# Two attentions on one core: the first group's Q and K, in halves by turns

## The chip, the cores and the metric

The kernel runs on one core of a Trainium2 chip. The metric is the device time in microseconds of one execution, as the median of several runs. Durations and waits come from one further execution, taken with the hardware profiler.

## The reference, cut to what matters

Two independent attention layers, A and B, each on 2048 tokens of 1024 features with 32 heads of 32, all in fp32. Both compute `qkv = x @ wqkv`, attention per head, and `o @ wo`; the outputs are put side by side.

```
B: scores = (q @ k.T) * Dh**-0.5 ; key in the last 256 tokens, else -1e9 ; softmax ; @ v ; @ wo
A: W, dil = 8, 2 ; idx = pos[:, None] - arange(W) * dil      # 8 keys, two tokens apart
   logits = einsum("bhsd,bhswd->bhsw", q, kg) * Dh**-0.5 ; masked ; softmax ; @ vg ; @ wo
```

In layer A a token only looks at tokens an even distance away, so the even and the odd tokens are two separate sequences of 1024, each with a window of 8 neighbours.

## The kernel before, in words

**Units and groups.** The work is cut into eight units of 512 tokens, `u` = 0 to 7. Units 0 to 3 are layer B (`DU` = 4, "dense"), units 4 to 7 are layer A. In each unit the 32 heads form eight groups of four, `s` = 0 to 7. A group's Q has 128 columns, and so has its K.

**Matmuls.** Every fp32 factor is split into a high and a low half (type fp32r): a cast gives the high half (L276 on ACT or L279 on DVE) and a subtraction on DVE the low one (L282). Each product then takes three matmuls (`TERMS`: high x high, high x low, low x high). Q or K of one group is a sum over eight blocks `k` of 128 features (`NK` = 8), so 24 matmuls of 512 columns into one PSUM bank. `qk_items` (L568) makes 16 items of three matmuls for a group, eight of Q and then eight of K; the last item of each evacuates its bank (L583 `evac_window` in layer A: L586 for Q, L591 for K). V is made by `v_items` (L728) in parts; the last part of a unit (two groups of heads) has 16 items on two banks, and its last two items copy these out to `vbuf` through `copy_out` (L718; L720 on ACT or L723 on DVE, whichever the planner holds to be sooner). In layer A, `window` (L1176) makes the scores of a group (128 small matmuls), the softmax on DVE and ACT (the band), eight copies of the turned band into `wide` (L1263, L1266) and the values block, whose result ACT copies at L1336.

**Banks and buffers.** Q, K, V and output products share a ring of three PSUM banks, tag `g` (`Ring`, L534; `psg` has 7 - `NS` = 3 buffers). A new product takes the next bank in turn, and its first matmul waits until the former content is evacuated. Weights lie in `wpool` (three buffers), x in `xpool` (nine tiles, each a high and a low half of one `k` block; a unit uses eight, two for each of four loads), raw loads in `raws` (three buffers).

**What sets the order.** One Python loop (at the end of the function) writes one program for all engines. It holds four lists: `gemm` (all items of Q, K, V and the output products, in a fixed order), scores, values and small auxiliary items. A `Clock` keeps planned times of every engine; at each step the loop takes the item whose planned start is earliest, a list of scores or values ahead of `gemm` when equal, and emits its instructions. What an item sets off on ACT, DVE, POOL and SP is emitted at that point or at a planned later time (`defer`). So the order on each engine follows from planned times, and on the chip each engine runs its program in that order, waiting on semaphores. Scores of the next group are released `P_LATE` = 1.5 us (planned) after the last copy of the band of the group before.

**Loads.** `Stream` (L177) holds one list of loads (`items`) in order of use. POOL issues each load into a raw buffer as soon as one is free (L221); `split_to` (L225) emits the cast and subtraction into the final tile. At the start of units 5 and 6 the list has: Q's weights of group 0, x quarters 0 and 1, K's weights of group 0, x quarters 2 and 3 (each quarter holds two of the eight `k` blocks). `x_items` (L1165) splits the four quarters; these four items are spliced among the 16 items of the last V part of the unit before, ahead of its items 1, 5, 9 and 13 (counted from 0), since they take over that unit's x tiles as V leaves them. In `run` of `qk_items` (L683) the items of K with `k` = 2 and `k` = 5 ask for the weights that come next.

The lines that a sentence can't say, from the loop that fills `gemm`:

```
            elif V_SLOTS.get(NG - 1) == p[2] and 0 < p[1] < U - 1:
                m = 2 * VPARTS[p[2]][1]
                for g, x in reversed(list(enumerate(x_items(p[1] + 1)))):
                    new[m * g + XAT:m * g + XAT] = x
```

Of the kernel before, what the change touches and what calls it, by code (L numbers as in the profile page):

```python
# [16 lines left out]
NK = 8  # L17
# [274 lines left out]
def kernel(ctx, tc, xs, wqk, wv, wo, outs, units):  # L292
# [3 lines left out]
    U = len(units)  # L296
    DU = sum(u[2] for u in units)
# [867 lines left out]
    def x_items(u):  # L1165
        xt[u], xready[u] = [], []

        def run(g):
            a, b = st.get(where["x", u, g])
            xt[u] += a  # L1170
            xready[u] += b

        return [[(lambda: 0.0, lambda g=g: run(g), 0.0, lambda: None)] for g in range(4)]
# [376 lines left out]
    def fill(at, n):  # L1550

        def run():
            mm(ps, idle[:, :P], idle, start=True, stop=True)

        def after(last):
            if last:
                rs.give(bank, ck.now + ck.SEM)

        return [(lambda: 0.0, run, CG, lambda i=i: after(at == FILL[-1][0] and i == n - 1)) for i in range(n)]
# [10 lines left out]
    for p in plan:  # L1570
        if not marks and p[1:] == (DU, 2) and p[0] == "qk":
            marks.append(len(gemm))
        if len(marks) == 1 and p[0] == "p":
            marks.append(len(gemm))
        if p[0] == "qk":
            new = qk_items(p[1], p[2])
            if p == ("qk", 0, 0):
                q, k, x = new[:NK], new[NK:], x_items(0)
                f = dict(FILL)
                new = x[0] + sum([q[i:i + 1] + fill(i + 1, f.get(i + 1, 0)) for i in range(4)], [])  # L1580
                for i in (1, 2, 3):
                    new[new.index(q[2 * i]) if i < 2 else len(new):0] = x[i]
                    if i == 1:
                        new += k[:4]
                    else:
                        new += q[2 * i:2 * i + 2] + k[2 * i:2 * i + 2]
            if p[1:] == (0, NG - 1):
                x1 = x1 or x_items(1)
                for g in range(3, FIRST_X - 1, -1):
                    new[NK + 2 * g - 2:NK + 2 * g - 2] = x1[g]  # L1590
            gemm += new
        elif p[0] == "v":
            new = v_items(p[1], p[2])
            if p[1:] == (0, 2) and FIRST_X:
                x1 = x_items(1)
                for g in range(FIRST_X - 1, -1, -1):
                    new[X1_AT[g]:X1_AT[g]] = x1[g]
# [4 lines that stand above are left out]
            gemm += new  # L1602
        elif p[0] == "o":
            gemm += o_items(p[1], p[2])
        elif p[0] == "p":
            gemm += product(p[1], p[2])
        elif p[0] == "vp":
            new = value_product(p[2])
            if VP_AT.get((p[1], NG - 1)) == p[2:] and p[1] + 1 < U:
                for g, x in reversed(list(enumerate(x_items(p[1] + 1)))):  # L1610
                    new[4 * g + XAT:4 * g + XAT] = x
            gemm += new
# [87 lines left out]
```

## Time and profile before

| | |
|---|---|
| median of 3 runs | 1789.3 us (1788.56 to 1789.42) |
| profiled execution, its own time | 1788.09 us |
| its span, first to last instruction | 1786.4 us |
| granted TensorE clock, mean | 1.000 |
| HBM read and written | 201.33 MB and 53.48 MB |
| bytes moved by DMA | 324.57 MB, mean 182 GB/s |

The profile page gives shares of the span for each engine: PE (matmuls), PEld (weight loads, which overlap them), DVE, ACT and POOL. Matmuls are pipelined and their ends are modelled, so two successive matmuls of 512 columns show a length of about 393 ns each but start closer together than that. A timeline row is: start in us from the start of the span, length in us, engine, source line, operation, output<-inputs by the program's names with sizes, count, and in brackets the idle time just before with what ended it. All matmuls have one line (L324, a helper), so they are told apart by names: `g<-x,w` of 512 columns are Q or K, `g<-w,x` are V (256 columns in the last part of a unit, 512 in the wide part), `s<-pbuf` the scores and `o<-wide,vbuf` the values of layer A. The stretches of this study are the starts of units 5 and 6, near 1144 and 1321 us of the span.

### The profile page before, as it was taken

Reading aid. Unit: us, or ns where it says so; the run is one execution under the profiler, and the core shown is the slowest. Engines: PE = TensorE matmul, PEld = TensorE weight load, DVE = VectorE, ACT = ScalarE, POOL = GpSimd, SP = SyncE. Lnnn points to the kernel's source line nnn. Section 1 sums busy time; section 2 is a strip of 40 time slices with the busy share of each in tenths; the row PEclk is TensorE's granted clock in tenths of the full one; section 3 lists DMA queues with packets and bytes.
Section 4 is the critical chain, followed back from the end, with each engine's and each line's share of the span. In section 5 each row is a group of like instructions: output and inputs, shape, how many; then the busy total and the mean of one; then the engine's idle time right before and its main releaser. Section 6 shows DMA issues by size and latency. Waiting matters only on the chain.

```text
span 1786.4 us, 38443 instructions
## 1 busy us (share of the span) xinstructions
PE 1768.4 (99%) x14496; PEld 1440.2 (81%) x14496; DVE 1295.5 (73%) x2881; ACT 936.9 (52%) x2332; POOL 412.8 (23%) x962
## 2 busy tenths in 40 slices
PE   9999999999999999999999999999999999999999
PEld 7787778888777888778788788878888887877887
DVE  6777876768867769867669546566577868767866
ACT  5565566555656565655654524444354546455442
POOL 3322324222333233242323410110011101001210
PEclk9999999999999999999999999999999999999999
DMA  8354664645645556555556255656576758948984
GB/s 256 106 151 136 187 167 137 163 135 152 186 142 154 154 127 173 150 148 156 133 142 186 72 181 180 210 193 209 175 219 197 233 169 290 303 151 271 310 319 144
DMA packets 154793, 324.57 MB, mean 182 GB/s; under 512 B 18032, under 2 KB 58992, under 8 KB 154608
## 3 DMA queue, kind: packets, MB, share of 16 engines
q0 software_dynamic: 45792, 166.74, 30.3%
q1 hardware_dynamic: 98736, 137.02, 26.9%
q10 hardware_dynamic: 10080, 18.35, 2.8%
q8 instruction: 115, 1.88, 0.4%
q14 instruction: 70, 0.57, 0.1%
HBM read 201.33 MB, written 53.48 MB: 143 GB/s over the span
## 4 chain that ended last, share of the span: by engine, by line
PE 92%; DVE 2%; DMA 2%; ACT 2%; issue 1%; SPq 0%; ACTq 0%; DVEq 0%; POOLq 0%
PE g L324 72%; PE s L324 13%; PE o L324 7%; DMA raw<-xs 1%; DVE w L282 1%; ACT s L1403 0%; DMA raw<-sd 0%; DMA pbuf<-nat 0%; DMA raw<-wqk 0%; DVE x L282 0%; ACT w L276 0%; DMA raw<-sx 0%; DMA qst<-nat 0%; ACT wide L1263 0%; ACT x L276 0%
## 5 line engine op out<-in xcount | busy, mean ns | idle before, releaser
L324 PE MATMUL g<-x,w 128*128 128x512 f32 x3552 | 875.8, 393 | 2.9 <-ACT x L276 1.0
L324 PEld LDWEIGHTS g<-x,w 128*128 128x128 f32 x3552 | 655.9, 188 | 131.7 <-issue 6.6
L282 DVE TENSOR_TENSOR w<-raw,w 128x512 fp32r<-128x512 f32 x510 | 334.3, 697 | 53.5 <-ACT w L276 47.2
L1398 DVE CUSTOM_DVE_ANT_0 s<-s,mask_d 128x384 f32<-128x384 f32 (+2 forms) x512 | 261.8, 554 | 98.4 <-PE s L324 98.1
L1403 ACT ACTIVATE s<-s,nm 128x384 f32<-128x384 f32 (+2 forms) x512 | 274.3, 537 | 109.9 <-DVE nm L1398 103.3
L324 PE MATMUL g<-w,x 128*128 128x256 f32 (+1 forms) x1728 | 306.9, 327 | 0.9 <-DVE w L282 0.7
L1462 POOL TENSOR_SCALAR_AFFINE_SELECT pbuf<-pbuf 128x128 f32<-128x128 f32 (+1 forms) x605 | 220.1, 392 | 315.7 <-ACT pbuf L1483 313.6
L324 PEld LDWEIGHTS g<-w,x 128*128 128x128 f32 x1728 | 255.3, 190 | 26.3 <-DVE w L282 2.2
L324 PE MATMUL g<-r,w 128*128 128x512 f32 x960 | 238.4, 393 | 0.5 <-DVE r L1362 0.5
L1483 ACT ACTIVATE pbuf<-s 128x384 f32<-128x384 f32 (+2 forms) x480 | 203.4, 504 | 65.3 <-PE s L324 63.5
L324 PEld LDWEIGHTS g<-r,w 128*128 128x128 f32 x960 | 177.2, 188 | 36.0 <-DVE r L1362 1.1
L221 POOL DMA_DIRECT2D raw<-wqk x126 | 68.4, 543 | 388.9 <-DVE w L282 265.2
L324 PEld LDWEIGHTS s<-qst,kst 128*128 128x128 f32 x704 | 113.5, 188 | 42.2 <-ACT s L1403 16.9
L324 PE MATMUL s<-kst,qst 96*128 96x384 f32 (+2 forms) x512 | 142.2, 342 | 0.9 <-ACT s L1403 0.7
L324 PE MATMUL s<-qst,kst 128*128 128x256 f32 (+2 forms) x704 | 137.0, 301 | 4.0 <-ACT s L1403 3.2
L279 DVE CAST w<-raw 128x1024 fp32r<-128x1024 f32 x176 | 121.3, 689 | 8.8 <-PE g L324 7.9
L324 PEld LDWEIGHTS s<-kst,qst 96*128 96x128 f32 x512 | 93.6, 189 | 26.2 <-issue 4.5
L276 ACT CAST w<-raw 128x1024 fp32r<-128x1024 f32 (+1 forms) x80 | 82.4, 1037 | 51.7 <-PE g L324 16.0
L1403 ACT ACTIVATION_READ_ACCUMULATOR s<-s,nm 128x1 f32 x512 | 105.3, 206 | 0.0
L1263 ACT COPY wide<-band 32x512 f32<-32x512 f32 x128 | 79.0, 617 | 30.3 <-DVE band L1254 28.8
L324 PE MATMUL o<-pbuf,vbuf 128*32 128x384 f32 (+2 forms) x1408 | 91.1, 388 | 0.0
L625 ACT ACTIVATE nat<-g 128x512 fp32r<-128x512 f32 x64 | 38.3, 598 | 97.7 <-PE g L324 87.1
(90 smaller groups left out, 1426.6 us busy)
## 6 DMA issues: line engine op xcount, KB each, us to landing
raw<-wqk POOLq DMA_DIRECT2D x126, 512.0 KB, 4.6
raw<-wv POOLq DMA_DIRECT2D x60, 512.0 KB, 4.8
qst<-nat SPq DMA_DIRECT2D x96, 256.0 KB, 4.2
kst<-nat SPq DMA_DIRECT2D x96, 256.0 KB, 5.5
raw<-wo POOLq DMA_DIRECT2D x44, 512.0 KB, 4.4
raw<-xs POOLq DMA_DIRECT2D x28, 512.0 KB, 4.5
kst<-halo SPq DMA_DIRECT2D x72, 128.0 KB, 4.5
pbuf<-nat SPq DMA_DIRECT2D x128, 65.0 KB, 3.2
```

The source lines that it names most:

```text
L221: (self.nc.scalar if early else self.nc.gpsimd).dma_start(raw if len(ap.shape) == 2 else raw.rearrange("p (a b) -> p a b", a=2), ap)
L276: nc.scalar.copy(t[:, 0, :], raw)
L279: nc.vector.tensor_copy(t[:, 0, :], raw)
L282: nc.vector.tensor_tensor(t[:, 1, c:c + 512], raw[:, c:c + 512], t[:, 0, c:c + 512].bitcast(F32), op=ALU.subtract)
L324: nc.tensor.matmul(out, left, right, **k)
L625: nc.scalar.activation(hl[:, 0, :], ps, AF.Copy, scale=sc)
L1263: nc.scalar.copy(diag[r:r + 32, :, :, c:c + 32], turned[r:r + 32, :, :, 1, :])
L1398: nc.vector.tensor_tensor_reduce(ps[:, :n], ps[:, :n], mask[:, cut:full], scale=-1.0, scalar=BIG, op0=ALU.add, op1=ALU.min, accum_out=nm)
L1403: nc.scalar.activation(ps[:, :n], ps[:, :n], AF.Exp, bias=nm, scale=-1.0, accum_out=sm)
L1462: nc.gpsimd.affine_select(w, w, pattern=[[0, m], [step, n]], compare_op=ALU.is_ge, fill=0.0, base=base, channel_multiplier=chan)
L1483: nc.scalar.activation(w, ps[:, :pack * n].rearrange("p (j n) -> p j n", j=pack), AF.Exp)
```

## The change

For the first group of heads (`s` = 0) of units 5 and 6, the 16 items of Q and K are put in another order: Q's `k` = 0 to 3, K's `k` = 0 to 3, Q's `k` = 4 to 7, K's `k` = 4 to 7. Two accumulations are then open at a time, in two banks. The items themselves, the loads and their order, and the places where x is spliced are as before.

```
                         new += q[2 * i:2 * i + 2] + k[2 * i:2 * i + 2]
+            if DU < p[1] < U - 1 and p[2] == 0:
+                new = [new[c + i] for h in (0, NK // 2) for c in (0, NK) for i in range(h, h + NK // 2)]
             if p[1:] == (0, NG - 1):
```

## The prediction

> **What bounds the kernel now.** I read the page first: busy shares, granted clock, chain by engine.
>
> ```profile
> PE 1768.4 (99%) x14496; PEld 1440.2 (81%) x14496; DVE 1295.5 (73%) x2881; ACT 936.9 (52%) x2332; POOL 412.8 (23%) x962
> PEclk9999999999999999999999999999999999999999
> PE 92%; DVE 2%; DMA 2%; ACT 2%; issue 1%; SPq 0%; ACTq 0%; DVEq 0%; POOLq 0%
> ```
>
> TensorE is busy 99% of the span and makes 92% of the chain. The change removes no matmul, so all it can alter is waits of TensorE, and of those only the few where layer A's second and third unit (u = 5 and 6) begin. I looked for these places in the timeline of PE and then of PEld. A row is: start, length, instruction, count, and in brackets the idle time ahead of it with its releaser.
>
> PE at the start of unit 5, then of unit 6:
>
> ```profile
> 1132.23 11.68 PE L324 MATMUL g<-w,x 128*128 128x256 f32 x96
> 1143.75 4.27 PE L324 MATMUL g<-x,w 128*128 128x512 f32 x18
> 1148.97 0.50 PE L324 MATMUL g<-x,w 128*128 128x512 f32 x1 [0.95 <-ACT x L276]
> 1149.97 6.90 PE L324 MATMUL g<-x,w 128*128 128x512 f32 x29 [0.51 <-DVE x L282]
> 1156.71 0.84 PE L324 MATMUL g<-w,x 128*128 128x512 f32 x3
> 1157.49 1.32 PE L324 MATMUL s<-pbuf 32*32 32x40 f32 x128
> 1158.73 1.12 PE L324 MATMUL o<-wide,vbuf 128*32 128x136 f32 x32
> 1159.79 2.58 PE L324 MATMUL g<-w,x 128*128 128x512 f32 x10
> 1162.84 17.34 PE L324 MATMUL g<-w,x 128*128 128x512 f32 x74 [0.47 <-DVE w L282]
> ```
> ```profile
> 1321.09 11.07 PE L324 MATMUL g<-x,w 128*128 128x512 f32 x48
> 1331.99 1.52 PE L324 MATMUL g<-w,x 128*128 128x512 f32 x6
> ```
>
> The 96 matmuls of 256 columns are V's last part of unit 4. Behind them stand 18 + 1 + 29 = 48 of g<-x,w: 24 of Q, then 24 of K, three for each of eight k-blocks. Unit 6 runs its 48 without a break, in 1331.99 - 1321.09 = 10.90 us, 0.227 each. Unit 5 needs 1156.71 - 1143.75 = 12.96, so it loses 2.06 us. It stops after 18 matmuls, that is ahead of Q's k = 6, whose x is the last fetched quarter: first for the ACT half (L276), then for the DVE half (L282). **The stall that the change aims at exists, once: 2.06 us at unit 5 and none at unit 6.**
>
> Next, ACT in the same places, since all that feeds or frees the matmuls here passes it:
>
> ```profile
> 1143.29 1.05 ACT L276 CAST w<-raw 128x1024 fp32r<-128x1024 f32 x1 [0.17 <-DMA raw<-wqk]
> 1144.47 1.14 ACT L276 CAST x<-raw 128x512 fp32r<-128x512 f32 x2
> 1148.30 1.14 ACT L276 CAST x<-raw 128x512 fp32r<-128x512 f32 x2 [2.68 <-DMA raw<-xs]
> 1149.34 1.06 ACT L720 COPY vbuf<-g 128x512 f32<-128x512 f32 x2
> 1151.44 0.60 ACT L586 ACTIVATE nat<-g 128x512 f32<-128x512 f32 x1 [1.04 <-PE g L324]
> 1151.94 0.60 ACT L1263 COPY wide<-band 32x512 f32<-32x512 f32 x1
> ...
> 1156.91 0.59 ACT L591 COPY nat<-g 128x512 f32<-128x512 f32 x1 [1.25 <-PE g L324]
> ...
> 1159.92 0.59 ACT L1336 COPY r<-o 128x512 f32<-128x512 f32 x1 [2.21 <-PE o L324]
> 1160.41 2.94 ACT L276 CAST w<-raw 128x1024 fp32r<-128x1024 f32 x3
> ```
> ```profile
> 1322.98 1.14 ACT L276 CAST x<-raw 128x512 fp32r<-128x512 f32 x2 [2.57 <-DMA raw<-xs]
> 1324.02 1.06 ACT L720 COPY vbuf<-g 128x512 f32<-128x512 f32 x2
> ```
>
> V's last matmul ends at 1132.23 + 11.68 = 1143.91, yet V's two banks are copied out (L720) only from 1149.34. ACT is not busy meanwhile: it sits idle 2.68 us for the DMA of the last x quarter, because the last quarter's item of x_items(u + 1) is spliced ahead of V's item 13 (of 0 to 15), so these two casts stand ahead of the copies in ACT's program. Unit 6 shows the same: idle 2.57, casts at 1322.98, copies at 1324.02.
>
> **The change, part by part.** No instruction is added or removed; 32 items of three matmuls are reordered, as Q k 0-3, K k 0-3, Q k 4-7, K k 4-7.
>
> *Q's k 4-7 later by 12 matmuls.* At unit 5 Q's k = 6 would come after 30 matmuls, 1143.75 + 30 x 0.227 = 1150.56, behind the 1149.97 at which its x is complete. That stall goes: at most -2.06 us.
>
> *K's k 0 earlier, and with it K's bank.* Here a new wait comes up. The ring of g banks has three (7 - NS). V's two blocks hold two, Q takes the third, so K's first matmul needs V's first bank, which the first L720 frees. Before, K began after Q's 24 matmuls, behind that copy. Now it is due after 12.
> - Unit 5: due at 1143.75 + 12 x 0.227 = 1146.47. The copy starts at 1149.34 and lasts half of the pair's row and a little (0.59), to 1149.93; from the end of the cast (1148.30 + 0.62) to the matmul that waited for it (1148.97) are 0.05 us, so K starts at about 1149.97. That is a wait of 3.5 us, with the rest of Q and K queued behind it in PE's order. By chance it is the instant at which the old kernel went on; but there 29 matmuls were left and here 36. Net **7 x 0.227 = +1.59 us**.
> - Unit 6: due at 1321.09 + 12 x 0.227 = 1323.81. The copy ends at 1324.02 + 0.58 = 1324.60, K starts at 1324.65: **+0.83 us**, where nothing was lost before.
>
> The other end for both is that the copy does not hold K: -2.06 and 0. I take the held value, since copies and casts are emitted before any of the moved items, so ACT's order up to there can't change. K's weights are no obstacle: cast at 1143.29 to 1144.34, their DVE halves done by the row below at 1145.66, ahead of 1146.47.
>
> ```profile
> 1144.37 1.29 DVE L282 TENSOR_TENSOR w<-raw,w 128x512 fp32r<-128x512 f32 x2 [0.45 <-ACT w L276]
> ```
>
> *What stands behind unit 5's K.* In the old order three matmuls of the next V part precede the score block (1157.49); then come the values block, ACT's copy of its result (1159.92), three weight casts (1160.41) and DVE's halves, for which PE waits until 1162.84. The planner releases the scores 1.5 us after the eight band copies (L1263, L1266). Q's evacuation (L586), ahead of those copies so far, falls behind them as Q ends later, so the scores come due by up to one evacuation (0.6 us) sooner, while K ends later in the plan. I expect the block right behind K, one V item (three matmuls, 0.69 us) earlier. The wait at 1162.84 hangs on the values block, so it moves by 1.59 - 0.69 = +0.90 and what PE does in between is absorbed. Bounds for unit 5 are +0.90 and +1.59; I take **+0.90**.
>
> *Nothing from the rest.* The next weights are asked for at K's k = 2 and 5, earlier in PE's order; Q's weight buffer comes free 12 matmuls later in the order, near 1155.4, and its next user is cast at 1160.41, five microseconds of cover. Q's bank is wanted again only after K and another block. The x tiles are read until K's k = 7, as before. On POOL and SP no DMA moves except the rows of Q and K, which go out as much later as their evacuation; the score block that reads them is a group away. Without that cover the price would be the shift itself, 1.6 us.
>
> *The sum.* +0.90 + 0.83 = +1.73 us. The profiled execution took 1788.09 us (span 1786.4, and 1.7 around it), so 1789.8 by its own time; the median of the three runs is 1789.3, 1.2 above, and gives **1791.0 us**, +0.10%.
>
> **The rivals.**
>
> *K is not held.* The copies come ahead of the casts, or the bank is another. Then -2.06 at unit 5 and nothing at unit 6: 1787.2. For it: the ring is small and I count its turns by hand. Against it: the 2.68 us of idle ACT between V's end and L720. Chance 0.10.
>
> *The loss is absorbed further on.* Where the chain of waits does not run through PE, a late PE costs nothing.
>
> ```profile
> 1471.65 7.68 issue
> 1479.33 0.01 POOLq L221
> 1479.35 4.60 DMA raw<-sx
> ```
>
> If this stretch starts from something other than PE, the 1.73 us are swallowed: 1789.3. Against it: PE is 149.72 of 150 us busy from 1350 to 1500, so there is little to swallow them.
>
> ```profile
> 1350.00:1500.00 150.00, 149.72 (x2018) 121.21 (x2016) 117.71 (x218) 74.94 (x142) 17.89 (x33) 1.00 0.68 210
> 1600.00:1786.40 186.40, 181.03 (x1294) 147.62 (x1292) 135.93 (x223) 82.89 (x133) 31.65 (x55) 1.00 0.76 259
> ```
>
> Chance 0.10.
>
> *The clock drops in the new gap (the slower side).* The longest idle time of PE around these places is 0.95 us, and the clock column stands at 1.00 throughout; the new gap at unit 5 would be 3.5 us from due to start, 3.1 without the last matmul's own 0.4. If the granted clock halved behind it, each matmul would cost 0.227 more. Eight of them take the sum past 0.2% (1.73 + 8 x 0.227 = 3.55); twelve, K's first half, give +2.7: 1793.7. Nothing in the trace speaks for it, as no such gap is in it. Chance 0.08. The Trainium skill, "TensorE: Matmul & The Clock Gate", section "Why this matters for your kernels", asks for no idle gap over about 3 us between bursts, since one idle window sends the clock to half. By it the gap is just at the edge; its window (3.4 us, in Part 1) at half speed would cost some 1.7 us more, an estimate from that page. No run here shows it.
>
> *The order behind it shifts.* The planner writes one order for all engines, and a changed due time may put score blocks or casts elsewhere for the rest. The price is bounded by waits that hang on that order: PE idles 186.40 - 181.03 = 5.4 us after 1600. Half as much again: +2.7 on the forecast, 1793.7, chance 0.14, and more, not less, if it hits several places; all of it gone: 1785.6, chance 0.04; no net effect, 0.02.
>
> **How the numbers follow.** Forecast 0.52 (with unit 5 between +0.90 and +1.59: 1791.0 to 1791.7). A difference below 0.2%, 3.6 us, is about what a measurement of this kernel can't tell from none. Slower by more: clock 0.08 and order 0.14, together 0.22. Faster by more: order 0.04. The same: 0.52 + 0.10 + 0.10 + 0.02 = 0.74. The range 1787.0 to 1794.0 takes in the free bank, the absorbed loss and the plain prices of clock and order, and leaves out the faster order and the upper part of the slower two.
>
> **What would show it.** In the changed trace, at unit 5: 12 matmuls of g<-x,w, a wait of about 3.5 us released by ACT vbuf L720, then 36 in one piece; no wait on x L276. At unit 6: 12, a wait of some 0.8 us on the same, then 36. ACT: still idle for raw<-xs ahead of L720; L586 behind the band copies. The score block right behind K. The clock at 1.00. I am wrong if K's first matmul follows Q's twelfth without a wait, if L720 stands ahead of the last casts, or if PE's busy time in the stretches behind 1350 moves by more than unit 5 and 6 do.

## The result, and the profile after

| | before | after |
|---|---|---|
| median of 14 runs each | 1788.57 us (1786.98 to 1791.97) | 1793.39 us (1790.58 to 1795.88) |
| ratio, 95% interval | | 1.0026 (1.0019 to 1.0033) |
| profiled execution, own time | 1788.09 us | 1794.82 us |
| its span | 1786.4 us | 1793.1 us |

The change costs 4.65 us by the ratio (3.4 to 5.9; the two medians lie 4.82 apart). The forecast was 1791.0, +1.73 us: the right sign and inside the range, but the loss is 2.7 times as large, and past the 0.2% behind which "the same" ended.

The page of after: busy time by engine, and the group of Q's and K's matmuls (busy time and mean ns of one | idle time ahead of them and what ended most of it).

```profile
PE 1771.4 (99%) x14496; PEld 1441.4 (80%) x14496; DVE 1294.8 (72%) x2879; ACT 939.1 (52%) x2334; POOL 411.7 (23%) x962
L324 PE MATMUL g<-x,w 128*128 128x512 f32 x3552 | 878.3, 393 | 5.4 <-ACT vbuf L720 4.0
```

All matmuls are still there. Of the 5.4 us for which Q and K kept PE idle, 4.0 now end with V's copy at L720, the release that the prediction named. DVE has two instructions fewer than before and ACT two more (2881 and 2332 then), so some of the planner's choices changed too.

PE of after at the start of unit 5, then of unit 6:

```profile
1143.74 2.91 PE L324 MATMUL g<-x,w 128*128 128x512 f32 x12
1149.35 10.05 PE L324 MATMUL g<-x,w 128*128 128x512 f32 x36 [2.71 <-ACT vbuf L720]
1159.24 0.84 PE L324 MATMUL g<-w,x 128*128 128x512 f32 x3
1160.02 1.32 PE L324 MATMUL s<-pbuf 32*32 32x40 f32 x128
...
1323.58 2.91 PE L324 MATMUL g<-x,w 128*128 128x512 f32 x12
1327.78 8.48 PE L324 MATMUL g<-x,w 128*128 128x512 f32 x36 [1.30 <-ACT vbuf L720]
1336.10 2.20 PE L324 MATMUL g<-w,x 128*128 128x512 f32 x9
1338.23 1.32 PE L324 MATMUL s<-pbuf 32*32 32x40 f32 x128
```

ACT of after in the same places:

```profile
1147.68 1.14 ACT L276 CAST x<-raw 128x512 fp32r<-128x512 f32 x2 [2.35 <-DMA raw<-xs]
1148.72 1.06 ACT L720 COPY vbuf<-g 128x512 f32<-128x512 f32 x2
1156.72 0.60 ACT L586 ACTIVATE nat<-g 128x512 f32<-128x512 f32 x1 [1.57 <-PE g L324]
...
1326.11 1.14 ACT L276 CAST x<-raw 128x512 fp32r<-128x512 f32 x2 [3.16 <-DMA raw<-xs]
1327.15 1.06 ACT L720 COPY vbuf<-g 128x512 f32<-128x512 f32 x2
```

The picture is the forecast one: twelve matmuls, a wait for L720, which stands behind casts that wait for x, then 36 in one piece. At unit 5 the first copy ends near 1148.72 + 0.59 = 1149.31, and K starts at 1149.35.

Two things were not forecast as likely. First, the 36 matmuls of unit 5 last 1159.24 - 1149.35 = 9.89 us, not 36 x 0.227 = 8.17. The windows of after tell why (length, then busy us and instructions of PE, PEld, DVE, ACT, POOL, then the granted clock, the DMA share and GB/s):

```profile
1149.30:1151.00 1.70, 1.65 (x5) 1.36 (x6) 1.70 (x3) 1.26 (x3) 0.46 (x1) 0.72 0.97 380
1151.00:1152.00 1.00, 1.00 (x4) 0.73 (x3) 1.00 (x3) 0.85 (x2) 0.26 (x1) 0.50 1.01 359
1152.00:1153.00 1.00, 1.00 (x4) 0.81 (x3) 0.60 (x2) 0.96 (x4) 0.00 (x0) 0.50 1.03 167
1153.00:1154.00 1.00, 1.00 (x4) 0.82 (x4) 0.00 (x0) 0.98 (x3) 0.72 (x1) 0.77 0.91 373
1154.00:1156.00 2.00, 2.00 (x10) 1.65 (x9) 0.00 (x0) 1.13 (x3) 0.00 (x0) 1.00 0.71 163
```

The clock fell to half some 0.7 us behind the gap and stayed there for about 3.4 us (0.28 x 1.7 / 0.5 + 2 + 0.23 / 0.5), which costs half of that, 1.7.

Second, more was lost behind unit 6. All waits of PE between 1345 and 1530, first before, then after:

```profile
1497.50 1.12 PE L324 MATMUL o<-wide,vbuf 128*32 128x136 f32 x32 [0.28 <-ACT wide L1266]
1501.76 0.58 PE L324 MATMUL s<-pbuf 32*32 32x40 f32 x41 [0.66 <-issue]
1515.69 0.50 PE L324 MATMUL g<-w,x 128*128 128x512 f32 x1 [0.19 <-DVE w L279]
1516.42 0.73 PE L324 MATMUL g<-w,x 128*128 128x512 f32 x2 [0.22 <-DVE w L282]
```
```profile
1477.62 2.37 PE L324 MATMUL g<-x,w 128*128 128x512 f32 x9 [0.66 <-issue]
1502.86 1.12 PE L324 MATMUL o<-wide,vbuf 128*32 128x136 f32 x32 [0.76 <-ACT wide L1266]
1507.46 0.57 PE L324 MATMUL s<-pbuf 32*32 32x40 f32 x40 [0.98 <-issue]
1515.03 5.29 PE L324 MATMUL g<-x,w 128*128 128x512 f32 x22 [0.21 <-DVE w L282]
1522.77 0.49 PE L324 MATMUL g<-w,x 128*128 128x512 f32 x1 [1.09 <-DVE w L279]
1523.49 0.73 PE L324 MATMUL g<-w,x 128*128 128x512 f32 x2 [0.23 <-DVE w L282]
```

The sums are 1.35 and 3.93 us. At unit 6, nine V matmuls stand ahead of the score block where six stood before, and from there on the planner's order differs on PE, ACT and DVE.

So the 6.7 us between the two profiled spans split in this way (from one row's start to another's, against before):

| stretch | before | after | difference |
|---|---|---|---|
| start to Q of unit 5 | 1143.75 | 1143.74 | 0 |
| unit 5, Q's start to the next V | 12.96 | 15.50 | +2.54, of which 1.72 from the clock |
| from there to Q of unit 6 | 164.38 | 164.34 | 0 |
| unit 6, Q's start to the next V | 10.90 | 12.52 | +1.62 |
| from there to the end | 454.41 | 457.0 | +2.6 |

This split is of one execution. The clock's part is larger in it than on average: each execution lists its mean granted clock (rounded to 0.001, that is 1.8 us), and (1 - clock) x time is a rough estimate of what it lost; it also counts a fall behind the last matmul, which costs nothing. Over its 14 runs after lost 1.4 us; for the runs of before beside them no clocks are on record, but in the three series of runs below the kernel before lost 1.1. By this estimate the average clock term is some +0.3 us, and most of the 4.65 us would be hold of K and new order. That is tested below.

### The profile page after: what moved, and what is told of

The parts are those of the page before. It is cut to its first block, busy times and chain, and to the rows that moved or that the text cites. A ratio compares the mean times of both kernels' runs of the same rounds, so it can differ in the third digit from the quotient of the medians.

```text
span 1793.1 us, 38435 instructions
## 1 busy us (share of the span) xinstructions
PE 1771.4 (99%) x14496; PEld 1441.4 (80%) x14496; DVE 1294.8 (72%) x2879; ACT 939.1 (52%) x2334; POOL 411.7 (23%) x962
## 4 chain that ended last, share of the span: by engine, by line
PE 91%; DMA 3%; DVE 2%; ACT 2%; issue 1%; SPq 0%; ACTq 0%; DVEq 0%; POOLq 0%
PE g L324 72%; PE s L324 13%; PE o L324 7%; DMA raw<-xs 1%; DVE w L282 1%; DMA raw<-sd 0%; ACT s L1403 0%; DMA pbuf<-nat 0%; DMA raw<-wqk 0%; DVE x L282 0%; ACT x L276 0%; DVE r L1010 0%; DMA qst<-nat 0%; DMA raw<-sx 0%; ACT w L276 0%
## 5 line engine op out<-in xcount | busy, mean ns | idle before, releaser
L282 DVE TENSOR_TENSOR w<-raw,w 128x512 fp32r<-128x512 f32 x510 | 334.4, 697 | 64.2 <-ACT w L276 58.0
L279 DVE CAST w<-raw 128x1024 fp32r<-128x1024 f32 x173 | 119.3, 689 | 9.4 <-PE g L324 8.5
```

What stands on the lines that cost most here:

```text
L279: nc.vector.tensor_copy(t[:, 0, :], raw)
L282: nc.vector.tensor_tensor(t[:, 1, c:c + 512], raw[:, c:c + 512], t[:, 0, c:c + 512].bitcast(F32), op=ALU.subtract)
```

## The experiments

My theory behind the result: K is held by V's copy at both units, the order behind unit 6 adds about as much again, and the clock falls behind the gap at unit 5. The rivals: it is all hold, or all order, or all clock. Each kernel was timed beside before on the same chip, in three series in which before's median was 1788.28, 1787.58 and 1787.50; the differences are of medians against before in the same series.

**Unit 5 alone.**

```
-            if DU < p[1] < U - 1 and p[2] == 0:
+            if p[1] == 5 and p[2] == 0:
```

> The turns by halves at unit 5 alone. Theory: K's first matmul waits there for V's copy behind the casts of the last x quarter, some 2.9 us instead of the old stall of 2.06, and the clock halves behind the gap in most executions (36 matmuls in 9.9 us, not 8.2). That is up to +2.5 us, about +1.0 in an execution whose clock holds: 1789.5 to 1791.1. Rival: the time comes from the new order of score blocks and casts behind unit 6, which this kernel does not have: 1788.6, as before.

Measured: 1790.46, ratio 1.0014 (1.0005 to 1.0023), +2.2 us; span 1786.6. PE of this kernel:

```profile
1143.46 2.91 PE L324 MATMUL g<-x,w 128*128 128x512 f32 x12
1148.99 8.45 PE L324 MATMUL g<-x,w 128*128 128x512 f32 x36 [2.62 <-ACT vbuf L720]
1157.28 0.84 PE L324 MATMUL g<-w,x 128*128 128x512 f32 x3
```

From Q to the next V it takes 13.82 us, +0.86: in this execution the hold is there and the clock stays full. Nine of its eleven executions list a mean clock below 1.000, with a mean loss of 2.8 us. With that taken off from the mean, and 1.1 from that of before, this kernel stands 0.9 above before. The profiled execution is the fastest of the eleven. Behind unit 6 PE's order in it is that of before, and the time from the V behind unit 6's K to the end is nearly the same: 454.06 us, against 454.41.

**Unit 6 alone.**

```
-            if DU < p[1] < U - 1 and p[2] == 0:
+            if p[1] == 6 and p[2] == 0:
```

> The turns by halves at unit 6 alone, which brings the new order behind it. Theory: K waits 0.8 to 1.5 us for V's copy there, and the order behind it costs the rest of the +4.8 us: about +2.3 in all, 1790.9, with the clock at 1.00 everywhere. Rival (order alone is the cause): +4 or more, 1792.6 and up. If the order is worth nothing: +0.8 to +1.5, 1789.4 to 1790.1.

Measured: 1791.97, 1.0021 (1.0012 to 1.0030), +3.7 us. Unit 6 itself takes 11.75 us, +0.85, with the wait on L720:

```profile
1323.99 8.48 PE L324 MATMUL g<-x,w 128*128 128x512 f32 x36 [0.52 <-ACT vbuf L720]
1510.09 5.31 PE L324 MATMUL g<-x,w 128*128 128x512 f32 x22 [0.92 <-DVE w L282]
1518.84 0.49 PE L324 MATMUL g<-w,x 128*128 128x512 f32 x1 [1.65 <-DVE w L279]
```

The other two rows are waits near 1515; all of PE's waits between 1345 and 1530 sum to 3.78, against 1.35 before. 0.85 + 2.43 = 3.3 us, near the 3.7 measured. The span of this execution is 4.8 us longer than that of before, since its clock also fell to half, behind the wait of 1.65 us, for about 1.7 us of loss; a clock of 1.00 everywhere had been expected. The unit without any stall in before costs most, and three quarters of the 3.3 us lie 190 us behind the edit.

**V's copies ahead of the last x casts, in both units,** in the kernel after (the last x item is put behind V's item 15, not ahead of item 13).

```
-                    new[m * g + XAT:m * g + XAT] = x
+                    at = len(new) if g == 3 and p[1] in (4, 5) else m * g + XAT
+                    new[at:at] = x
```

> The changed kernel with the split of the last x quarter of units 5 and 6 put behind V's last item, so that V's two copies stand ahead of these two casts on ACT. Theory: K's first matmul follows Q's twelfth without a wait at both units, the old stall of 2.06 us is gone, the clock holds; what is left is the new order behind unit 6 (+0 to +2.6): 1786.5 to 1789.1. Rival (K is held by something else, such as its weights or the DMA of x): the waits stay, 1793.4.

Measured: 1789.29, 1.0003 (0.9995 to 1.0012), +1.0 us. PE and ACT of this kernel at unit 5:

```profile
1143.41 11.07 PE L324 MATMUL g<-x,w 128*128 128x512 f32 x48
1154.32 0.84 PE L324 MATMUL g<-w,x 128*128 128x512 f32 x3
```
```profile
1145.17 1.06 ACT L720 COPY vbuf<-g 128x512 f32<-128x512 f32 x2
1146.99 1.14 ACT L276 CAST x<-raw 128x512 fp32r<-128x512 f32 x2 [0.76 <-DMA raw<-xs]
```

With the copies first, all 48 matmuls run without a break in 10.91 us, 2.05 less than before, as the change seems to promise. So the hold is due to the place of L720. Still the kernel is not faster: from the start of unit 6 to the end it takes 467.0 us (before: 465.3), and that is most of what unit 5 gained. PE's order behind unit 6 is here that of after, and the waits between 1345 and 1530 sum to 3.88, as in after.

**The same move of the copies, without the change.**

```
-            if DU < p[1] < U - 1 and p[2] == 0:
-                new = [new[c + i] for h in (0, NK // 2) for c in (0, NK) for i in range(h, h + NK // 2)]
...
+                    at = len(new) if g == 3 and p[1] in (4, 5) else m * g + XAT
+                    new[at:at] = x
```

> The kernel before with V's copies ahead of the casts of the last x quarter at units 5 and 6, and Q and K as they were. Theory: K begins behind Q's 24 matmuls, when its bank has long been free, so the copies are on no path: 1788.3, the stall of some 2 us at unit 5 stays. Rival (the copies cost the casts their place, or a free bank helps by itself): a change of 0.5 us or more.

Measured: 1788.69, 1.0004 (0.9996 to 1.0013), +1.1 us. The old stall stays (12.87 us at unit 5). The copies alone make no difference that these runs can tell from none; a small one, up to some 2 us, is not excluded.

**The gap at unit 5 filled** with eleven matmuls into a score bank, whose result nobody reads, in the kernel after.

```
+                if (u, s, t, k) == (5, 0, 0, 3):
+                    ps, bank = rs.take()
+                    for _ in range(11):
+                        nc.tensor.matmul(ps, h["w"][:, 0, :P], xt[u][0][:, 0, :], start=True, stop=True)
+                    rs.give(bank, ck.now)
```

> The changed kernel with 11 matmuls more into an idle bank of the scores' ring between Q's first half and K's first half of unit 5 (their result is never read), so that TensorE works through the wait for V's copy. Theory (the clock gate): the clock stays at 1.00 in 1149 to 1154, the 36 matmuls behind take 8.2 us instead of 9.9, and the time falls by up to 1.7 us from that of the changed kernel: about 1791.9. Rival (the slow matmuls come from the crowded DMA and SBUF in that stretch): still some 9.9 us, no change, 1793.4.

Measured: 1792.77, 1.0025 (1.0016 to 1.0033), +4.5 us. PE of this kernel:

```profile
1146.34 2.66 PE L693 MATMUL s<-x,w 128*128 128x512 f32 x11
1148.83 8.32 PE L324 MATMUL g<-x,w 128*128 128x512 f32 x36
```

There is no gap any more, the 36 matmuls take 8.16 us, and the mean clock loss is 0.65 us, less than the 1.1 of before. The time didn't fall to the 1791.9 expected all the same: with no more clock loss than before has, 4.5 us are left. That speaks against a theory in which the clock makes up the surplus over the forecast, but it is no clean test, since the filling shifts PE's work: unit 6 loses only 0.20 here, as its x came early enough, and PE stops on nothing that the profile names at 1318.99 (0.54 us) and 1626.44 (1.21).

**The same filling with unit 5 alone, and unit 5 alone once more beside it.**

```
+                if (u, s, t, k) == (5, 0, 0, 3):
...
-            if DU < p[1] < U - 1 and p[2] == 0:
+            if p[1] == 5 and p[2] == 0:
```

> The turns by halves at unit 5 alone, with 11 matmuls more into an idle bank of the scores' ring while K waits for V's copy (their result is never read). Theory (an idle gap of some 2.7 us lets the clock fall in a part of the executions): the clock's mean loss falls back to that of the kernel before, about 1.1 us, and only the wait itself is left, +0.9: 1.7 us less than its partner without the filling. Rival (the clock falls for another reason, as it does at times in the kernel before): same clocks and same time as its partner.

> The turns by halves at unit 5 alone once more, as the partner on the same chip of the next kernel: some 2.5 us above the kernel before, with the granted clock below 1.000 in most executions (a mean loss of about 2.8 us against 1.1 in the kernel before).

Measured: filled 1790.51, 1.0017 (1.0008 to 1.0026), +3.0 us; not filled 1788.56, 1.0007 (0.9998 to 1.0016), +1.1 us. The clock stayed full in the profile of the latter too, behind the longest gap of all:

```profile
1149.74 8.46 PE L324 MATMUL g<-x,w 128*128 128x512 f32 x36 [2.93 <-ACT vbuf L720]
```

Only two of its eleven executions list a clock below 1.000 (loss 0.5 us), where nine of eleven did in the first series on another chip. So the expectation for the unfilled kernel (some +2.5 us, the clock below 1.000 in most executions) was missed. The filled kernel is slower, not faster, and its trace shows waits of PE on nothing that the profile names:

```profile
1319.76 3.02 PE L324 MATMUL g<-w,x 128*128 128x256 f32 x24 [1.04 <-issue]
1505.06 0.67 PE L324 MATMUL s<-pbuf 32*32 32x40 f32 x52 [1.21 <-issue]
```

With two more at 1340 (1.20) and 1625 (1.07) these are 4.5 us behind 1300, where its partner has a single one of 0.67. Whether the filling brings them isn't shown: with the change at both units such waits sum to 1.75 us behind 1300 with the filling and to 1.64 in after without it. With only 0.5 us lost to the clock in the partner, the pair can't price the clock. What the unfilled one does show is that the gap doesn't always bring a fall.

**After's instructions in before's order.** The planner's choice among its four lists is replaced by the recorded choices of before, so that PE's order differs from before's in the 32 items alone.

```
...
-            if t is not None and (best is None or max(t, ck.now) < best[0]):
+            if t is not None and name == turns[turn]:
                 best = max(t, ck.now), name
...
+        turn += 1
```

> The changed kernel, but with the turns of the four lists (products, scores, values, small items) as the kernel before took them, given as a list instead of by planned times. So units 5 and 6 have the halves, and TensorE's order is otherwise the old one. Theory (hold of K at both units, and the new order worth about +3): the time falls back to the hold alone, +2.2 from unit 5 and +0.5 to 0.8 from unit 6: 1791.0 or a little less. Rival (the order behind is worth nothing): 1793.4.

Measured: 1790.53, 1.0020 (1.0011 to 1.0030), +2.95 us; the profiled execution is the fastest of the ten (1788.72, span 1787.0). PE of this kernel at units 5 and 6:

```profile
1148.73 8.45 PE L324 MATMUL g<-x,w 128*128 128x512 f32 x36 [2.27 <-ACT vbuf L720]
...
1324.63 8.46 PE L324 MATMUL g<-x,w 128*128 128x512 f32 x36 [0.53 <-ACT vbuf L720]
```

Unit 5 takes 13.46 us (+0.50), unit 6 11.74 (+0.84): a hold of 1.34 us. Behind unit 6 the cost of the order is gone: PE's waits between 1345 and 1530 sum to 1.35 us, as in before, and from the V behind unit 6's K to the end it takes 454.07 us (before: 454.41, after: 457.0). The list fixes the turns, not every engine: here and in the next kernel ACT has one instruction more than in before and DVE one less, since the planner still chooses which of them makes a copy or cast.

**Before in after's order.** The reverse: Q then K as before, but after's recorded choices.

```
-            if DU < p[1] < U - 1 and p[2] == 0:
-                new = [new[c + i] for h in (0, NK // 2) for c in (0, NK) for i in range(h, h + NK // 2)]
...
-            if t is not None and (best is None or max(t, ck.now) < best[0]):
+            if t is not None and name == turns[turn]:
...
```

> The kernel before, with Q and K as they were, but with the turns of the four lists as the changed kernel took them. It has the old stall at unit 5 and no hold of K. Theory: the new order by itself costs some 3 us: 1791.3, with PE idle for some 3 us in 1500 to 1600 instead of 1.1. Rival: the order costs nothing by itself and only hurts together with the late units: 1788.3.

Measured: 1791.02, 1.0021 (1.0013 to 1.0030), +3.4 us, without one item of Q or K exchanged. PE's waits of this kernel between 1345 and 1530:

```profile
1473.16 2.23 PE L324 MATMUL g<-x,w 128*128 128x512 f32 x9 [0.64 <-issue]
1498.29 1.12 PE L324 MATMUL o<-wide,vbuf 128*32 128x136 f32 x32 [0.76 <-ACT wide L1266]
1503.03 0.56 PE L324 MATMUL s<-pbuf 32*32 32x40 f32 x39 [1.11 <-issue]
1518.19 0.49 PE L324 MATMUL g<-w,x 128*128 128x512 f32 x1 [1.09 <-DVE w L279]
1518.91 0.73 PE L324 MATMUL g<-w,x 128*128 128x512 f32 x2 [0.23 <-DVE w L282]
```

These are after's waits, one by one but for the 0.21 on w L282, 3.83 us in all, 2.5 more than before's 1.35. From the start of unit 6 to the end this kernel takes 468.2 us, before 465.3: +2.9. The order alone costs about what after lost behind its hold at unit 6 (+2.6). Not all of these waits belong to it: the one inside the score block near 1503 (1.11 here, 0.98 in after, 0.66 in before) is 0.94, 0.98 and 1.12 in three kernels with the old order too (unit 5 alone, copies alone, after in old order). Up to 0.5 us of the 2.5 may therefore be no price of the order. The time from the V behind unit 6's K to the end separates the two orders without overlap: 454.0 to 454.4 in before and these three, 456.1 to 457.3 in after, copies first and before in new order (458.9 in unit 6 alone, with 1.7 of it from the clock).

**Copies first at unit 5 alone,** with the change at unit 5 alone (`p[1] == 5`, and `p[1] == 4` for the copies).

```
+            if p[1] == 5 and p[2] == 0:
...
+                    at = len(new) if g == 3 and p[1] == 4 else m * g + XAT
...
```

> The halves at unit 5 alone, with V's copies ahead of the casts of the last x quarter there, and nothing else changed: no new order behind. Theory: the old stall of 2.06 us goes and nothing comes in its place: 1786.2. Rival (the stretch behind unit 5 gives the gain back, since the weights of the next V part come no sooner): 1787.5 to 1788.3.

**Copies first at both units, in before's order.** The third experiment's edit with the sixth's.

```
+                    at = len(new) if g == 3 and p[1] in (4, 5) else m * g + XAT
...
+            if t is not None and name == turns[turn]:
```

> The halves at units 5 and 6, with V's copies ahead of the casts of the last x quarter there (no hold of K), and the turns of the four lists as in the kernel before (no new order). Theory: only the gain of the change is left, the old stall of 2.06 us: 2.0 us below the kernel before, if no later wait takes it back; like the version at unit 5 alone, whose profile lost 0.6 of it in the score block behind, so -1.3 to -2.0. Rival: no difference from the kernel before.

Measured: 1787.95, 0.9997 (0.9988 to 1.0006), +0.4 us, and 1786.78, 0.9995 (0.9986 to 1.0004), -0.7 us. Both run their 48 matmuls in 10.90 us, yet neither can be told from before. The gain of 2 us that the theories gave is not shown; but the intervals (-2.1 to +1.1 and -2.5 to +0.7 us) don't exclude it. PE of the second one, and a window:

```profile
1144.03 11.07 PE L324 MATMUL g<-x,w 128*128 128x512 f32 x48
1159.15 0.29 PE L324 MATMUL s<-pbuf 32*32 32x40 f32 x12 [2.23 <-issue]
```
```profile
1161.00:1163.00 2.00, 2.00 (x6) 1.52 (x5) 0.88 (x2) 2.00 (x3) 0.00 (x0) 0.50 0.21 73
```

In this execution the 2.06 us gained are gone at once: PE stops 2.23 us inside the score block, on nothing that the profile names, and the clock falls behind it. But it is the second slowest of the eleven, so it need not be typical. The first one shows a stop behind the same 116 matmuls of the block (0.61 us). Where the stop comes from was not found. In the third experiment, with the same copies and no such stop, the gain of unit 5 was still there at unit 6 (its Q starts at 1318.81, before's at 1321.09).

The profiled execution of the first one, the slowest of its eleven, has a fall of the clock too, 970 us ahead of the edit (PE, then a window):

```profile
168.26 1.84 PE L324 MATMUL s<-qst,kst 128*128 128x384 f32 x4 [0.97 <-ACT s L1403]
170.00:180.00 10.00, 10.00 (x52) 7.56 (x51) 5.81 (x17) 5.75 (x17) 4.97 (x12) 0.83 0.35 107
```

The same wait of 0.97 us stands there in all thirteen traces, before's included, and in the other twelve the clock stays at 1.00 behind it.

## Why the prediction was right in sign and short in size

**The hold of K: right, and of the right size.** The wait on L720 is there in every kernel that has the change and keeps the copies behind the casts (or the filling stands in its place), and gone in the three that put the copies first; only at unit 6 of the filled kernel x came early enough to leave 0.20 us without a wait. Unit 6 was priced at +0.83 and measured +0.85 and +0.84 alone and in the old order. In after it was 1.62: x's last quarter was cast 3.13 us later than before while PE was only 2.49 later. That the copy hangs on a DMA, which doesn't shift along with PE, was not in the sum. Unit 5 was priced at +0.90, with bounds to +1.59; the kernels with a full clock there measured +0.50, +0.86 and +1.18 (14.14 us in the repeat), and after 2.54 - 1.72 = +0.82. Together, +0.86 and +0.85 make 1.71 of the 1.73 forecast; with unit 5 anywhere from +0.50 to +1.18, an agreement this close is luck.

**The failed step: "Nothing from the rest".** The sum set the order behind unit 6 at zero and kept it as a rival with 0.14, at +2.7 on top. By before in after's order it costs +2.9 in the trace and +3.4 (2.3 to 5.4) in the median. Hold and order make 1.7 + 2.9 = 4.6 us; the measured loss is 4.65. The sign of being wrong that the text named is there too: PE's busy time falls by 0.4 us in 1350 to 1500 and by 2.2 in 1500 to 1600, more than the 1.73 forecast for units 5 and 6 (but less than the 4.16 that the two took in this trace). The mechanism of that rival was right: the waits that grew (L279, L282, L1266, issue) are of the kinds that PE already had. Its place was not: it bounded them by the idle time after 1600, and they grew between 1470 and 1525. And the chance looks low, since the text itself said that one planned time changes the order for all engines.

**"Nothing is absorbed": right.** From unit 5 to unit 6 the trace carries the whole delay, 164.34 against 164.38 us. **"The score block one V item earlier": wrong.** At unit 5 three V matmuls stay ahead of it, and the order there is before's; at unit 6 it came one item later. L586 did fall behind the band copies, but brought no score block forward. So the 0.69 us taken off for that was wrong, and +0.82 came near +0.90 by luck: the last x quarter was cast 0.62 us earlier (1147.68, not 1148.30), and K started as much earlier.

**The clock: it happens, in a part of the executions.** This rival (0.08) came true in the profiled execution of after, 1.72 us at unit 5, but not in those of the two unit-5 kernels, with gaps of 2.62 and 2.93. (Eight slowed matmuls would not take the sum past 0.2%, as the text has it: its 3.55 us is just under 3.6.) The Trainium skill, "TensorE: Matmul & The Clock Gate", Part 1, says that the window of 3.4 us by which the clock is judged runs freely and isn't set off by the kernel. The half-clock stretch of about 3.4 us agrees with its length, and a phase that differs from run to run could let the clock fall behind a gap of 2.7 us and not behind one of 2.9; no run here shows the phase. The falls stand behind gaps of 0.97 to 2.71 us, all less than the 3 us of the rule that the prediction cited.

**Open.** After in the old order measured +2.95 where its trace shows a hold of 1.34; with +3.4 for the order the two sum to 6.4, more than after's 4.65. Each has an interval of about 1.6 us to either side, and by the clock estimate the former lost 0.8 us more to the clock than before did and the latter 1.0. Taken off, that leaves 2.1 and 2.5, together 4.6; but the estimate is rough (the profiled execution of the latter lists 0.999, and its clock falls only behind the last matmul), so the rest isn't settled. What the issue waits come from is open too. And whether a gap causes the falls of the clock is argued from their place, not shown: filling it changed other things, and one fall stands behind a gap that other executions pass at full clock.

## What to carry to other kernels

When accumulations are interleaved, ask first which bank the second one takes and where the instruction that empties it stands in its engine's program: here a copy behind casts that wait for a DMA cost more than the stall that the swap removed. Where a planner writes the order, a local swap has a second price, paid far behind it; record the planner's choices and run each half by itself (old items in the new order, new items in the old one) before explaining the total. And look for a gain in the median, not only at its place: with the hold gone and the order kept, unit 5 is 2.06 us shorter, but one profiled execution lost as much again within five microseconds, and the median (-0.7 us) can't be told from no gain.

## What the runs showed of the hardware

- Four falls of the clock to half were profiled ahead of the last matmul, and each cost about 1.7 us. They stood behind gaps of PE of 2.71 us (after), 2.23 (both mended), 1.65 (unit 6 alone) and 0.97 (unit 5, copies first), while gaps of 2.93, 2.62 and 2.27 left it at 1.00. So the length of the gap alone doesn't decide it. Even before, 99% busy, loses an estimated 1.1 us per execution on average.
- One kernel (unit 5 alone) lost an estimated 2.8 us to the clock in the series on one chip and 0.5 in that on another.
- PE also stops on nothing that the profile names, 0.2 to 2.2 us at a time, mostly inside or at the end of blocks of small matmuls. Eleven more matmuls and their weight loads in one place went with 4.5 us of such stops against 0.67 in one pair of traces, and with 1.75 against 1.64 in another.
